# C-B products of units 4 to 7 in two row groups in turn, the second in the bank of y, under new due times

## The chip, the core and the metric

The kernel runs on one core of a Trainium2 chip. Five engines work from queues of their own: TensorE (PE in the profile, PEld its weight loads), VectorE (DVE), ScalarE (ACT), GpSimd (POOL) and SyncE (SP, which issues all DMAs here). The metric is the device time of one execution in microseconds; less is better.

## What is computed

Three stages in a row, all in fp32 at the interface. A chunked linear scan ("attention") over 4 batches, 8 heads, 768 steps; then an MLP with an ELU; then a second MLP in which two products are multiplied by each other.

```python
# scan, per chunk; cum = cumulative log decay in the chunk
CB = einsum('bhin,bhjn->bhij', Cc, Bc)          # the C-B product
M = CB * L                                      # L = exp(cum_i - cum_j), causal
y = einsum('bhij,bhjd->bhid', M, xc) + einsum('bhin,bhnd->bhid', Cc, state) * exp(cum)
state = decay_full * state + sum_j Bx_j
# MLP 1: 3072 tokens, 256 -> 2048 -> 256
h = x @ w_in;  g = where(h > 0, h, exp(min(h, 0)) - 1);  x = g @ w_out
# MLP 2: 3072 tokens, 256 -> 1536 -> 256
x = ((x @ w_a) * (x @ w_b)) @ w_out2
```

## The kernel before

**Units.** The scan is cut into 24 units, u = 0 to 23, one for 128 steps of one batch. Four units make one token tile of 512 (n = u // 4, also called t in the MLP), and eight make a set s = u // 8. A unit has these steps, all in the function `unit`: loads by SP (`ld_*`); the scan of decays on DVE (`scan`, L630); the last column to `le` (`last_col`, L645, L647) and x times it on POOL (`xend`, L650); the C-B product on PE; `mask`, C-B times the decay matrix, on DVE (L686), once for each half of four heads; M, the product with x and with the state on PE (`ym`, L717, L721, L725), into `ybank`, the bank of y; the state's update (`st_up`, L739, L741); and y out of the bank as x of the MLP, on ACT and DVE (`x_w`, L757, for tile 0; `x_hi`, L760, and `x_lo`, L763, from tile 1 on).

**C-B in three forms.** Units 0 to 3 (n == 0) use `cbm2`: heads 0 to 3 stand on rows 0 to 15 of the operand tile and heads 4 to 7 on rows 32 to 47, so that the two groups use different rows of the array; their matmuls alternate, and each group has its own PSUM bank. Units 4 to 7 (s == 0, n == 1) have the same operands (fp32, 16 rows) but use `cbm` once for each group: 4 matmuls, which are 8 passes of the array in fp32, into `cbank`, and the mask of a group must have read the bank before the next one writes. Units 8 to 23 use `cbm` on bf16 operands of 128 rows, which ACT casts (L531) and SP stores (L539) and loads again (L578).

**The bank of y** holds y of a unit in columns 0 to 255, the two tiles of the new state (`dsb`) in 256 to 383, and in the last 128 the target of the fillers: `warm` (L369), bf16 matmuls of zeros.

**MLP 1.** Tile 0 uses the weights in plain fp32 (L783, two passes a matmul). From tile 1 on each fp32 value is split into two fp32r parts, and a product is three matmuls (L792, L793, L795 for up, L804, L805, L808 for down). The work goes in pairs of 128 hidden columns: up into one of two up tiles of two banks (`up_115`, `up_116` in the rows, pairs alternate), exponential on ACT (`ex`, L890), minus one (`em`, L894), the ELU's choice on DVE (`gg`, L900, into `e_86` and others), hi and lo parts (`hi` L904, `lo` L909 on DVE or L911 on POOL), then down into two accumulators (`acc_117`, `acc_118`). Pair p+2 writes the up tile of pair p. MLP 2 goes in groups (L1120 to L1253).

**What sets the order.** All steps are put into a list by `add`, with a planned cost on one or more engines, the steps they follow, and a due time. `Plan.emit` runs a list schedule over it: among the steps that could start, it takes the earliest start, then the earliest due time, and issues the step on the engine chosen. The result is a fixed order on each engine. The table MOVE shifts due times by part ("unit", 4) and step ("cbm"). Where PE would stand idle by the plan before FILL_TO = 50 us, `emit` puts in fillers through `plan.fill`. On the chip each engine follows its order and waits on semaphores.

Of the kernel before, what the change touches and what calls it, by code (L numbers as in the profile page):

```python
# [17 lines left out]
P = 128  # L18
# [31 lines left out]
    ("bc", (0, 2, 1)): {"": 3.2, "rest": -2.7},  # L50
    ("bc", (1, 2, 0)): {"rest": 2.4},
    ("late", 1): {"rest": -2.9},
    ("late", 3): {"": -1.4, "comb": 1.7, "high_s": 3.6},
    ("late", 4): {"": 2.6, "high": 2.5},
    ("late", 6): {"": -5.0, "comb": 3.2},
    ("late", 8): {"": -20},
    ("pair", (1, 3)): {"": -2.5},
    ("pair", (3, 3)): {"": -1.3},
    ("pair", (3, 5)): {"": 1.0},
    ("pair", (3, 6)): {"": 0.6},  # L60
    ("pair", (4, 0)): {"": -2.1},
    ("split", ("w_in", 2)): {"": -4.1},
    ("split", ("w_in", 3)): {"": 5.8},
    ("split", ("w_out", 0)): {"high": -1.3},
    ("split", ("w_out", 1)): {"high": 5.2},
    ("split", ("w_out", 3)): {"": -1.3},
    ("unit", 0): {"scan": -2.0},
    ("unit", 1): {"ld_x": 2.0},
    ("unit", 10): {"": 5.1, "ld_x": -0.4, "x_lo": -0.4},
    ("unit", 11): {"st_up": 0.1},  # L70
    ("unit", 12): {"": 7.3, "ld_sm": 1.4, "mask": 4.4},
    ("unit", 13): {"": -3.7},
    ("unit", 14): {"ld_sm": -1.5},
    ("unit", 15): {"": 1.6, "<lambda>": -1.2, "xend": 4.0, "ym": 4.4},
    ("unit", 16): {"cbm": 0.8, "st_bd": 1.3},
    ("unit", 17): {"x_lo": 4.1},
    ("unit", 18): {"<lambda>": -5.5},
    ("unit", 19): {"cbm": 0.5},
    ("unit", 2): {"scan": -0.3},
    ("unit", 20): {"": -4.2, "<lambda>": -1.0, "st_bd": -1.1},  # L80
    ("unit", 21): {"": 7.1, "mask": -5.0, "scan": 2.8},
    ("unit", 22): {"": 2.7, "ld_sm": -1.6, "ld_x": 1.7},
    ("unit", 23): {"": 1.9, "ld_a": 2.0, "scan": 1.7},
    ("unit", 3): {"cbm": 2.6, "last_col": 3.1, "mask": -0.9},
# [3 lines left out]
    ("unit", 9): {"": -3.0, "st_up": -3.3},
    ("w", ("w_in", 0)): {"sign": -1.0},
    ("w", ("w_in", 2)): {"put": -2.4},  # L90
    ("w", ("w_in", 3)): {"load": -1.7},
    ("w", ("w_out", 1)): {"sign": -0.6},
    ("w", ("w_out", 2)): {"": 2.4},
    ("wb", ("w_a", 0)): {"last3": -1.1},
    ("wb", ("w_a", 1)): {"": 7.0},
    ("wb", ("w_a", 2)): {"load": -5.3, "scale": 3.3, "sign": 0.4},
    ("wb", ("w_b", 2)): {"": 2.4},
    ("wb", ("w_out2", 1)): {"": 3.2, "put": 4.0, "shift": -3.9},
    ("wb", ("w_out2", 2)): {"": 6.1, "shift": 1.8},
    ("xset", 1): {"": 11.1},  # L100
    ("xset", 2): {"": 10.6, "f_t3": -8.8, "x_h": 1.6, "x_l": 6.0},
# [1336 lines left out]
```

## Time and profile before

| | us |
|---|---|
| median of 3 runs | 628.99 (628.84 to 629.89) |
| the profiled execution | 627.92 |
| its span | 626.2 |
| PE busy | 619.4 |
| DVE, ACT, POOL busy | 392.6, 372.4, 342.8 |

The profiled execution is one run by itself; its span leaves out what lies around the first and the last instruction on the engines. In a timeline an instruction's time begins when it enters the engine and its end is modelled, so of back-to-back matmuls the distance from one start to the next is the cost, and the second column, which counts the last one's drain, is a little more.

### The profile page before, as it was taken

How to read it: one execution, taken by the hardware profiler on the slowest of the kernel's cores; microseconds unless marked ns; L12 is line 12 of the kernel's file. 1: busy time of each engine (PE TensorE's matmuls, PEld its weight loads, DVE VectorE, ACT ScalarE, POOL GpSimd, SP SyncE). 2: the span in 40 equal slices, each digit the busy share in tenths (PEclk: the TensorE clock that was granted, in tenths of full speed). 3: DMA queues.
4: the chain of work that ended last, by engine and by line, in shares of the span. 5: the costliest groups of instructions: out<-in, count | busy, mean ns of one | idle time of the engine just before them, and what ended most of it. 6: DMA issues, size and time to landing. Idle time of an engine off the chain costs nothing. (4 is left out here: it accounts for less than half of the span.)

```text
span 626.2 us, 9495 instructions
## 1 busy us (share of the span) xinstructions
PE 619.4 (99%) x3658; PEld 485.3 (77%) x3658; DVE 392.6 (63%) x525; ACT 372.4 (59%) x528; POOL 342.8 (55%) x260
## 2 busy tenths in 40 slices
PE   9999999999999999999999999999999999999997
PEld 8955556788777788777888888888888888788885
DVE  7876686787876987887753766346533446433333
ACT  2375747647676776756678655557544456554443
POOL 2233465246764586546637476557655666555552
PEclk9999999999999999999999999999999999999999
DMA  6968622657668766410000000000100000100001
GB/s 194 337 198 268 208 66 92 223 173 269 214 201 299 269 211 188 152 51 1 1 1 0 2 0 1 0 1 1 68 0 2 2 0 1 68 2 0 1 0 68
DMA packets 33405, 59.96 MB, mean 96 GB/s; under 512 B 2736, under 2 KB 13904, under 8 KB 33360
## 3 DMA queue, kind: packets, MB, share of 16 engines
q1 hardware_dynamic: 33360, 59.35, 28.9%
q8 instruction: 29, 0.48, 0.3%
q14 instruction: 16, 0.13, 0.1%
HBM read 47.61 MB, written 11.73 MB: 95 GB/s over the span
## 5 line engine op out<-in xcount | busy, mean ns | idle before, releaser
L1209 DVE TENSOR_TENSOR x<-x 128x512 f32<-128x512 f32 x36 | 31.7, 884 | 82.5 <-POOL x L1253 82.0
L911 POOL TENSOR_TENSOR gl<-e,gh 128x1024 fp32r<-128x1024 f32 x20 | 50.9, 2545 | 29.1 <-ACT gh L904 21.9
L1215 POOL TENSOR_TENSOR gl<-x,gh 128x512 fp32r<-128x512 f32 x35 | 48.8, 1395 | 32.9 <-ACT gh L1212 32.9
L1253 POOL TENSOR_TENSOR x<-e,x 128x512 f32<-128x512 f32 x36 | 46.3, 1304 | 31.6 <-ACT e L1192 29.4
L804 PE MATMUL acc<-gh,hi_w_out 128*128 128x512 f32 x160 | 63.4, 396 | 0.0
L805 PE MATMUL acc<-gh,lo_w_out 128*128 128x512 f32 x160 | 62.4, 390 | 0.0
L890 ACT ACTIVATE e<-up 128x1024 f32<-128x1024 f32 x44 | 45.1, 1024 | 26.2 <-PE up L795 18.8
L630 DVE TENSOR_TENSOR_SCAN ab<-ab,delta 128x512 f32<-128x512 f32 x36 | 53.6, 1514 | 0.0
L808 PE MATMUL acc<-gl,hi_w_out 128*128 128x512 f32 x160 | 51.3, 397 | 0.1
L894 ACT ACTIVATE e<-e,bias 128x1024 f32<-128x1024 f32 x44 | 50.7, 1153 | 1.0
L900 DVE SCALAR_TENSOR_TENSOR up<-e,up 128x512 f32<-128x512 f32 x40 | 27.7, 692 | 24.8 <-ACT e L894 24.1
L1215 POOL TENSOR_TENSOR gl<-p,gh 128x512 fp32r<-128x512 f32 x18 | 23.9, 1327 | 30.8 <-issue 25.9
L792 PE MATMUL up<-xh,hi_w_in 128*128 128x512 f32 x96 | 39.4, 410 | 0.6 <-DVE gl L909 0.6
L1200 DVE TENSOR_TENSOR p<-acc,p 128x512 f32<-128x512 f32 x36 | 24.6, 690 | 24.5 <-PE acc L1182 23.2
L900 DVE SCALAR_TENSOR_TENSOR e<-e,up 128x512 f32<-128x512 f32 x48 | 30.7, 679 | 11.6 <-ACT e L894 11.4
L1121 PE MATMUL up<-gh,lo_w_out 128*128 128x512 f32 x96 | 37.5, 391 | 0.0
L793 PE MATMUL up<-xh,lo_w_in 128*128 128x512 f32 x96 | 37.5, 390 | 0.0
L1120 PE MATMUL up<-gh,hi_w_out 128*128 128x512 f32 x96 | 37.4, 390 | 0.0
L493 POOL TENSOR_TENSOR m<-m,raw 128x1024 int32<-128x1024 int32 x10 | 26.0, 2605 | 16.9 <-DVE m L483 13.9
L805 PEld LDWEIGHTS acc<-gh,lo_w_out 128*128 128x128 f32 x160 | 30.1, 188 | 5.9
L804 PEld LDWEIGHTS acc<-gh,hi_w_out 128*128 128x128 f32 x160 | 30.0, 188 | 5.9
L686 DVE TENSOR_TENSOR ab<-cbank,ab 128x512 f32<-128x512 f32 x37 | 25.3, 683 | 13.4 <-PE cbank L683 12.6
(306 smaller groups left out, 1731.9 us busy)
## 6 DMA issues: line engine op xcount, KB each, us to landing
ab<-a_seg SPq DMA_DIRECT2D x18, 512.0 KB
parts<-raw SPq DMA_DIRECT2D x64, 128.0 KB
sm<-parts SPq DMA_DIRECT2D x16, 512.0 KB
p<-in_xb SPq DMA_DIRECT2D x20, 256.0 KB
raw<-in_w_out SPq DMA_DIRECT2D x4, 1024.0 KB
fx<-in_w_out SPq DMA_DIRECT2D x3, 1024.0 KB
out_t<-m SPq DMA_DIRECT2D x12, 256.0 KB
raw<-in_w_in SPq DMA_DIRECT2D x2, 1024.0 KB
```

The lines of the kernel that those rows point to most:

```text
L630: nc.vector.tensor_tensor_scan(lt[:, h4].rearrange(flat), lt[:, h4].rearrange(flat) if n else flat4(sp[g]), delta.rearrange(flat), 0.0, op ...
L792: nc.tensor.matmul(ps, w_mm(name, whi, f, c), xh[:, c, :], start=(c == 0), stop=False)
L793: nc.tensor.matmul(ps, w_mm(name, wlo, f, c), xh[:, c, :], start=False, stop=False)
L804: nc.tensor.matmul(accs[m], w_mm(name, whi, f, m), gh, start=(f == 0), stop=False)
L805: nc.tensor.matmul(accs[m], w_mm(name, wlo, f, m), gh, start=False, stop=False)
L808: nc.tensor.matmul(accs[m], w_mm(name, whi, f, m), gl, start=False, stop=(f == last))
L890: nc.scalar.activation(gf, u, AF.Exp)
L894: nc.scalar.activation(gf, gf, AF.Identity, bias=bias[:, 0:1])
L900: nc.vector.scalar_tensor_tensor(u[:, k, :] if on_dve else gf[:, k, :], gf[:, k, :], 0.0, u[:, k, :], op0=ALU.min, op1=ALU.max)
L911: nc.gpsimd.tensor_sub(gl.ap, gf, gh.ap.bitcast(F32))
L1215: eng[e].tensor_sub(tap("l" + w), tap(wa), tap("h" + w).bitcast(F32))
L1253: eng[e].tensor_add(tap(w), tap(v), tap(w))
```

## The change

Units 4 to 7 take `cbm2` too. The second group's bank is that of y, so the step takes (waits for) the users of `cbank`, of the bank of y and of both state tiles in it; the masks of the second group read the bank of y. When unit 4's C-B is issued, fillers end. The planned costs of several PE steps are changed, and MOVE is replaced altogether: its 52 entries go and 96 others come (two shown of each). The arithmetic is the same.

```diff
 MOVE = {
-    ("unit", 4): {"": 1.9, "cbm": -3.5, "mask": 0.4},
-    ("unit", 7): {"": 1.6, "ym": -2.8},
...
+    ("unit", 4): {"cbm2": 20, "mask": -6.7},
+    ("unit", 8): {"": -1.6, "<lambda>": 3.2, "ld_a": 1.9, "ld_x": 9.7, "scan": -5.7},
...
-        i_cbs = None
-        if n == 0:
+        if s == 0:
+
+            if n:
+                cb_ = [cbb, yb]
+            cap = [flat4(x) for x in cb_]
 
             def cbm2(e):
+                if n:
+                    plan.fill = None
                 for h in range(4):
                     for g in range(2):
                         q = slice(h * P, (h + 1) * P)
                         t = sm32[row + 32 * g:row + 32 * g + N]
-                        nc.tensor.matmul(flat4(cb_[g])[:, q], t[:, 0, q], t[:, 1, q], start=True, stop=True)
-
-            i_cbs = add({"PE": 0.95}, cbm2, cb_[0].take(), cb_[1].take(), i_sm, due=due, weight=0.25)
+                        nc.tensor.matmul(cap[g][:, q], t[:, 0, q], t[:, 1, q], start=True, stop=True)
+
+            old = cb_[0].take() + cb_[1].take() + (dsb[0].users + dsb[1].users if n else [])
+            i_cbs = add({"PE": 1.1 if n == 0 else 1.25}, cbm2, old, i_sm, due=due, weight=0.25)
             smu.users.append(i_cbs)
+        else:
+            cb_ = [cbb, cbb]
         for g in range(2):
             h4 = slice(4 * g, 4 * g + 4)
 
-            cb = cb_[g] if n == 0 else cbb
-
-            def cbm(e, g=g, cbank=cb.ap):
+            def cbm(e, g=g):
                 for h in range(4):
-                    if s == 0:
-                        q = slice(h * P, (h + 1) * P)
-                        t = sm32[row + 32 * g:row + 32 * g + N]
-                    else:
-                        q = slice((4 * g + h) * P, (4 * g + h + 1) * P)
-                        t = sm.ap
-                    nc.tensor.matmul(cbank[:, h, :], t[:, 0, q], t[:, 1, q], start=True, stop=True)
+                    q = slice((4 * g + h) * P, (4 * g + h + 1) * P)
+                    nc.tensor.matmul(cbank[:, h, :], sm.ap[:, 0, q], sm.ap[:, 1, q], start=True, stop=True)
...
-            if n:
-                i_cb = add({"PE": 0.28 if s else 0.88}, cbm, cb.take(), i_sm, due=due, pad=pd, weight=1.0 if s else 0.125)
+            if s == 0:
+                i_cb = i_cbs
+            else:
+                i_cb = add({"PE": 0.31}, cbm, cbb.take(), i_sm, due=due, pad=pd)
                 smu.users.append(i_cb)
...
-                i1.append(add({"PE": 0.86}, dn_w, i_h, i_m[wk], d, i1, due=due))
+                i1.append(add({"PE": 0.92}, dn_w, i_h, i_m[wk], d, i1, due=due))
...
-            i_u.append(add({"PE": 0.88}, up_h, d_u, i_u, i_x[t][2 * q:2 * q + 2], i_m["w_in", 0],
+            i_u.append(add({"PE": 0.92}, up_h, d_u, i_u, i_x[t][2 * q:2 * q + 2], i_m["w_in", 0],
...
-                i_u.append(add({"PE": 1.72}, up_a, d_u, i_u, i_x[t], i_m[wk], due=due + 0.1 * k))
+                i_u.append(add({"PE": 1.84}, up_a, d_u, i_u, i_x[t], i_m[wk], due=due + 0.1 * k))
```

The table has 44 rows more, so a line of the new file stands some 44 to 49 lines further down: L666 of before is L715, L717 is L762, L721 is L766, L783 is L828, L792 is L837, L890 is L935, L369 is L413. PE has 176 fillers instead of 190: in the old order the last 12 stand ahead of pair 2's up, in the new order the last 18 stand between M of unit 3 and the first full up, and none follows.

PE at pair 2's up (`m_104` is the second quarter of w_in), the order before, from the end of the fillers:

```order
L783 MATMUL up_115<-x_93,m_104 128x512 x2
L683 MATMUL cbank<-sm_76 128x128 x4
L783 MATMUL up_115<-x_93,m_104 128x512 x2
L783 MATMUL acc_117<-e_86,m_103 128x512
L783 MATMUL acc_118<-e_86,m_103 128x512
L717 MATMUL ybank<-p_74,sbd 32x128 x4
L721 MATMUL ybank<-f_hi_w_out_99,p_74 32x128 x4
L717 MATMUL ybank<-p_74,sbd 32x128 x4
L721 MATMUL ybank<-f_hi_w_out_99,p_74 32x128 x4
L725 MATMUL ybank<-xe,p_74 32x64 x4
```
and in the changed kernel, from the last two of unit 4's C-B matmuls:

```order
L715 MATMUL cbank<-sm_76 128x128
L715 MATMUL ybank<-sm_76 128x128
L828 MATMUL up_115<-x_93,m_104 128x512 x4
L762 MATMUL ybank<-p_74,sbd 32x128 x4
L766 MATMUL ybank<-f_hi_w_out_99,p_74 32x128 x4
L762 MATMUL ybank<-p_74,sbd 32x128 x4
L766 MATMUL ybank<-f_hi_w_out_99,p_74 32x128 x4
L770 MATMUL ybank<-xe,p_74 32x64 x4
L828 MATMUL acc_117<-e_86,m_103 128x512
L828 MATMUL acc_118<-e_86,m_103 128x512
```
Unit 4's C-B (8 matmuls that alternate between `cbank` and `ybank`) stands whole ahead of that up, where the second half stood in its middle; its first half stood ahead of the first full up.

ACT at the exponentials of pair 0 (`up_115` to `e_86`); `m_105` is a part of w_out whose scaling is one step. Before:

```order
L890 ACTIVATE e_86<-up_115 128x1024
L894 ACTIVATE e_86<-e_86,bias 128x1024
L645 COPY le_82<-f_hi_w_out_99 128x8
L475 ACTIVATE m_105<-raw_72 128x1024
L890 ACTIVATE e_87<-up_116 128x1024
```
and in the changed kernel:

```order
L935 ACTIVATE e_86<-up_115 128x1024
L519 ACTIVATE m_105<-raw_72 128x1024
L939 ACTIVATE e_86<-e_86,bias 128x1024
L689 COPY le_82<-f_hi_w_out_99 128x8
L532 ACTIVATE raw_72<-raw_72 128x1024
L935 ACTIVATE e_87<-up_116 128x1024
```
The scaling of `m_105` has moved between the exponential of pair 0 and the step behind it.

SP at the start of the program (`sm`: C-B operands, `p`: x of a unit, `raw_72` the first weight quarter). Before:

```order
L588 DMA sm_76<-in_bc 16x1024 x2
L571 DMA p_74<-in_xb 128x512
L466 DMA raw_72<-in_w_in 128x2x1024
L588 DMA sm_76<-in_bc 16x1024 x2
L571 DMA p_75<-in_xb 128x512
```
and in the changed kernel:

```order
L632 DMA sm_76<-in_bc 16x1024 x2
L615 DMA p_75<-in_xb 128x512
L632 DMA sm_76<-in_bc 16x1024 x2
L615 DMA p_74<-in_xb 128x512
L510 DMA raw_72<-in_w_in 128x2x1024
```
The second unit's x is loaded ahead of the first one's, and the first weight load comes behind all four instead of the first two.

## Rows read from the trace of the kernel before

**Rows 1.** The page: busy us (share of the span) x instructions; tenths in 40 slices.
```profile
PE 619.4 (99%) x3658; PEld 485.3 (77%) x3658; DVE 392.6 (63%) x525; ACT 372.4 (59%) x528; POOL 342.8 (55%) x260
...
PE   9999999999999999999999999999999999999997
...
PEclk9999999999999999999999999999999999999999
```

**Rows 2.** Waits of PE: engine, line, releaser; total us, times, longest us.
```profile
PE ybank L369 <- POOL zt L365: 1.1, 1, 1.1
PE up L792 <- DVE gl L909: 0.6, 1, 0.6
PE up L1124 <- POOL gl L1215: 0.4, 1, 0.4
PE cbank L683 <- DVE ab L686: 0.2, 1, 0.2
```

**Rows 3.** Timeline of PE, 30 to 84 us: start us, us, engine, line, operation, tiles, count.
```profile
30.49 1.15 PE L683 MATMUL cbank<-sm 16*128 16x128 f32 x8
31.57 5.43 PE L783 MATMUL up<-x,m 128*128 128x256 f32 x16
36.84 0.83 PE L369 MATMUL ybank<-zt 128*128 128x128 bf16 x12
37.51 1.94 PE L783 MATMUL up<-x,m 128*128 128x512 f32 x4
39.37 1.15 PE L683 MATMUL cbank<-sm 16*128 16x128 f32 x8
40.46 1.98 PE L783 MATMUL up<-x,m 128*128 128x512 f32 x4
...
48.21 3.70 PE L783 MATMUL up<-x,m 128*128 128x512 f32 x8
51.84 1.15 PE L683 MATMUL cbank<-sm 16*128 16x128 f32 x8
...
61.63 3.60 PE L783 MATMUL up<-x,m 128*128 128x512 f32 x8
65.16 1.15 PE L683 MATMUL cbank<-sm 16*128 16x128 f32 x8
...
82.78 1.15 PE L683 MATMUL cbank<-sm 16*128 16x128 f32 x8
83.86 1.12 PE L783 MATMUL acc<-e,m 128*128 128x512 f32 x2
```

**Rows 4.** Groups of PE, 30 to 90 us: busy us, mean ns, idle before.
```profile
L683 PE MATMUL cbank<-sm 16*128 16x128 f32 x64 | 9.2, 283 | 0.0
```

**Rows 5.** Timeline of PE, 11 to 14 us: unit 0's C-B and the next step.
```profile
11.38 1.16 PE L666 MATMUL up<-sm 16*128 16x128 f32 x16
12.47 1.72 PE L606 MATMUL acc<-a,delta 128*128 128x128 f32 x13
```

**Rows 6.** Timeline of ACT, then of DVE, 32 to 38 us: pair 0's gate, a mask.
```profile
33.60 1.02 ACT L890 ACTIVATE e<-up 128x1024 f32<-128x1024 f32 x1 [2.49 <-PE up L783]
34.66 1.15 ACT L894 ACTIVATE e<-e,bias 128x1024 f32<-128x1024 f32 x1
...
35.81 1.16 ACT L475 ACTIVATE m<-raw 128x1024 f32<-128x1024 f32 x1
...
32.57 1.22 DVE L630 TENSOR_TENSOR_SCAN f_hi_w_out<-f_hi_w_out,delta 128x512 f32<-128x512 f32 x1
35.84 1.28 DVE L900 SCALAR_TENSOR_TENSOR e<-e,up 128x512 f32<-128x512 f32 x2 [2.05 <-ACT e L894]
37.04 0.68 DVE L686 TENSOR_TENSOR f_hi_w_out<-cbank,f_hi_w_out 128x512 f32<-128x512 f32 x1
```

**Rows 7.** Timeline of PE at its three later waits, and what follows.
```profile
174.31 0.38 PE L683 MATMUL cbank<-sm 128*128 128x128 bf16 x4 [0.18 <-DVE ab L686]
...
203.70 0.47 PE L792 MATMUL up<-xh,hi_w_in 128*128 128x512 f32 x1 [0.63 <-DVE gl L909]
204.00 0.39 PE L793 MATMUL up<-xh,lo_w_in 128*128 128x512 f32 x1
...
533.18 0.73 PE L1124 MATMUL up<-gl,op_x 128*128 128x512 f32 x2 [0.44 <-POOL gl L1215]
```

**Rows 8.** Timeline of PE, ACT, DVE, 45 to 47 us: y of unit 4.
```profile
44.98 0.29 PE L725 MATMUL ybank<-xe,p 128*32 128x64 f32 x8
45.21 1.98 PE L783 MATMUL acc<-e,m 128*128 128x512 f32 x4
...
45.66 0.34 ACT L760 CAST xh<-ybank 128x256 fp32r<-128x256 f32 x1
...
46.03 0.28 DVE L741 SCALAR_TENSOR_TENSOR state<-state,db,ybank 128x64 f32<-128x64 f32 x1
46.23 0.42 DVE L763 TENSOR_TENSOR xl<-ybank,xh 128x256 fp32r<-128x256 f32 x1
```

**Rows 9.** Timeline of PE, first 10.3 us: fillers L369, spread of unit data L606.
```profile
1.06 3.49 PE L369 MATMUL ybank<-zt 128*128 128x128 bf16 x31 [1.06 <-POOL zt L365]
4.34 3.02 PE L606 MATMUL acc<-a,delta 128*128 128x128 f32 x16
...
8.38 2.05 PE L606 MATMUL acc<-a,delta 128*128 128x128 f32 x16
10.27 0.50 PE L369 MATMUL ybank<-zt 128*128 128x128 bf16 x6
```

**Rows 10.** Timeline of ACT, SP, PE, 99 to 115 us: unit 8's operands.
```profile
103.15 0.61 ACT L531 CAST raw<-raw 128x512 bf16<-128x512 f32 x1
...
99.52 5.45 SPq L539 DMA_DIRECT2D parts<-raw  x8
107.85 0.90 SPq L578 DMA_DIRECT2D sm<-parts  x2
...
114.46 0.40 PE L683 MATMUL cbank<-sm 128*128 128x128 bf16 x4
```

**Rows 11.** Windows of 1 us: length, busy (x) by engine, PEclk, DMA share, GB/s.
```profile
109.00:110.00 1.00, 1.00 (x6) 0.82 (x5) 1.00 (x3) 0.97 (x2) 0.00 (x0) 1.00 0.37 127
110.00:111.00 1.00, 1.00 (x6) 0.84 (x5) 1.00 (x1) 0.76 (x1) 0.00 (x0) 1.00 1.03 401
```

More of the change, by code (lines that the diff above doesn't have):

```diff
@@ L49 @@
 MOVE = {
[L50 to L84, printed above, removed]
-    ("unit", 4): {"": 1.9, "cbm": -3.5, "mask": 0.4},
@@ L86 @@
-    ("unit", 5): {"x_lo": -2.4},
-    ("unit", 7): {"": 1.6, "ym": -2.8},
[L88 to L101, printed above, removed]
+    ("bc", (0, 1, 0)): {"": 1.4, "load": -1.3},
+    ("bc", (0, 2, 1)): {"": -11.6},
+    ("bc", (1, 2, 0)): {"": -9.3, "rest": 3.7},
+    ("bc", (1, 2, 1)): {"rest": -8.8},
+    ("group", 0): {"": -5.3, "dn_h": 1.5, "mm3": 0.3},
+    ("group", 10): {"": -1.9, "gg": 0.4},
+    ("group", 11): {"": -5.7},
@@ new lines @@
+    ("group", 12): {"": 2.5},
+    ("group", 2): {"": 1.7},
+    ("group", 3): {"": -3.9, "dn_h": -1.1, "gg": 5.6},
+    ("group", 4): {"mm3": 2.6},
+    ("group", 5): {"dn_h": 0.8, "mm3": 1.6},
+    ("group", 6): {"mm3": -1.9},
+    ("late", 2): {"": -17.0, "high": -5.8},
+    ("late", 3): {"high_s": 11.9},
+    ("late", 5): {"": -14.2},
+    ("late", 6): {"": -11.4, "rest": -17.5},
+    ("late", 7): {"": 6.3, "high": -10.0},
+    ("late", 8): {"": -0.9},
+    ("pair", (0, 2)): {"gg": -3.3},
+    ("pair", (0, 4)): {"": 0.9, "up_a": -6.9},
@@ new lines @@
+    ("pair", (0, 5)): {"dn_w": 1.6},
+    ("pair", (0, 6)): {"dn_w": 3.0},
+    ("pair", (0, 7)): {"dn_w": 1.6},
+    ("pair", (1, 0)): {"dn_w": -2.6},
+    ("pair", (1, 5)): {"": 1.2, "up_a": -0.6},
+    ("pair", (2, 0)): {"": -12.7, "hi": -1.1},
+    ("pair", (2, 1)): {"up_a": -2.0},
+    ("pair", (2, 2)): {"dn_h": 2.2, "lo": -2.2},
+    ("pair", (2, 4)): {"dn_h": -1.2},
+    ("pair", (2, 6)): {"up_a": -2.2},
+    ("pair", (2, 7)): {"": -3.4, "up_a": -3.6},
+    ("pair", (3, 0)): {"": -2.7, "dn_h": -0.9},
@@ new lines @@
+    ("pair", (4, 6)): {"dn_h": 7.0},
+    ("pair", (5, 1)): {"dn_0": 3.5, "up_a": 1.1},
+    ("pair", (5, 2)): {"dn_l": 2.2, "up_a": 2.0},
+    ("pair", (5, 3)): {"": -0.8, "em": 0.5},
+    ("pair", (5, 4)): {"up_a": -10.4},
+    ("pair", (5, 5)): {"dn_l": -0.5},
+    ("pair", (5, 6)): {"dn_h": 3.2},
+    ("pair", (5, 7)): {"dn_l": -1.9},
+    ("split", ("w_in", 0)): {"rest": -1.6},
+    ("split", ("w_in", 1)): {"high": 4.4},
+    ("split", ("w_in", 2)): {"": 4.7, "high": -0.1, "rest": 4.8},
+    ("split", ("w_in", 3)): {"high": -0.3},
@@ new lines @@
+    ("split", ("w_out", 0)): {"": 1.8},
+    ("split", ("w_out", 1)): {"": 12.0, "rest": -2.8},
+    ("split", ("w_out", 2)): {"": 10.7},
+    ("unit", 0): {"": -5.5, "ld0": 5.7, "ld_x": 8.5},
+    ("unit", 1): {"": -11.1},
+    ("unit", 11): {"x_lo": -0.5, "ym": -8.7},
+    ("unit", 12): {"": -19.7, "scan": 20},
+    ("unit", 13): {"": -17.6, "ld_x": 14.8},
+    ("unit", 14): {"": -10.3, "<lambda>": 2.5, "ld_x": -20},
+    ("unit", 15): {"": 1.8, "ld_db": -7.4, "scan": -10.0},
+    ("unit", 17): {"<lambda>": -4.0, "cbm": 6.4, "xend": -7.2},
@@ new lines @@
+    ("unit", 18): {"": -3.2, "scan": 3.5, "st_bd": 2.1, "x_lo": 15.0},
+    ("unit", 19): {"<lambda>": -5.2, "scan": 1.5, "st_up": 5.3},
+    ("unit", 21): {"": 4.7, "cbm": -3.4, "scan": 1.0, "st_bd": 10.4, "ym": 5.0},
+    ("unit", 22): {"cbm": -4.9},
+    ("unit", 23): {"": 5.7, "cbm": 9.6, "ld_x": -3.7},
+    ("unit", 3): {"st_up": -3.1},
+    ("unit", 4): {"cbm2": 20, "mask": -6.7},
+    ("unit", 5): {"<lambda>": 1.1, "ld_a": 5.3},
+    ("unit", 6): {"": -5.4},
+    ("unit", 7): {"": 2.4},
@@ new lines @@
+    ("unit", 8): {"": -1.6, "<lambda>": 3.2, "ld_a": 1.9, "ld_x": 9.7, "scan": -5.7},
+    ("unit", 9): {"": 3.0, "ld_a": 2.1, "scan": -5.9},
+    ("w", ("w_in", 0)): {"last3": -9.8},
+    ("w", ("w_in", 1)): {"": -4.9},
+    ("w", ("w_in", 2)): {"": -2.3, "shift": -3.8, "sign": 5.7},
+    ("w", ("w_in", 3)): {"": -2.1, "load": 1.4},
+    ("w", ("w_out", 0)): {"": -19.9, "load": 1.2},
+    ("w", ("w_out", 1)): {"last3": 13.0, "put": -5.6, "sign": -6.4},
+    ("w", ("w_out", 2)): {"": 1.6},
+    ("w", ("w_out", 3)): {"": 5.8, "load": -3.8},
```

28 lines of the change are left out of this document (23 added, 5 removed).

## The prediction

> **What bounds the kernel now.** I began with the page: TensorE (PE) is busy in 99% of the span and no other engine in more than 63% [rows 1]. The next view was PE's waits by releaser, which asks whether its 1% is worth anything: four waits, 2.3 us in all, 1.1 of it before the first instruction has data [rows 2]. So time can leave this kernel almost only with PE's own instructions or with the gaps between them, and the PE timeline was read next. The span is 626.2 and the profiled execution took 627.92; the rest of 1.7 us lies around it, and the tail behind the last matmul has the same order in both kernels. All sums below are against 627.92, and are then set on the median of the runs, 628.99, which is 1.07 higher.
>
> In the timeline one thing stands out between 30 and 84 us. A C-B block of units 4 to 7 (8 passes of 16 rows, one row group, one bank) takes 1.15 us and the next instruction starts 1.08 to 1.09 behind it: 30.49 to 31.57, 39.37 to 40.46, 82.78 to 83.86 [rows 3]. There are 8 such blocks, 64 instructions [rows 4]. Ahead of them the trace shows the other form: unit 0's C-B goes to both row groups in turn, two banks, 16 passes, and the next instruction starts 1.09 behind it, 11.38 to 12.47 [rows 5]. Twice the passes cost the same time, since two stand in the array at once. Mean of one is 283 ns in the slow form while they are issued at 1.09/8 = 136 ns; in the alternating form 68 ns.
>
> **The change part by part.**
>
> *Blocks.* Eight blocks become four of 16 passes: 8 × 1.085 − 4 × 1.09 = 4.3 us of PE time gone.
>
> *Switches.* The array must change its form of tiling on both sides of a block. Eight L783 passes between two blocks last 3.63 (48.21 to 51.84), and 3.53 with a block on one side only (61.63 to 65.16) [rows 3]; so one side costs 0.10, a block 0.20, and four blocks fewer give 0.8. Together a block fewer is worth 1.28, four are worth 5.1.
>
> *Fillers.* 190 become 176, and none stands behind unit 4's C-B any more, because the bank of y is in use there. Fillers are issued where PE would wait anyway, so I cost them at nothing: the cover is the wait itself. The 12 at 36.84 lasted 0.67 and stood ahead of the pair-2 up, which needs pair 0's gate product out of its bank: that ended at 37.12, and the up started at 37.51 [rows 3, 6]. If all 14 were pure loss, 14 × 0.056 (0.67/12) = 0.8 would be gained: an end of the range.
>
> *The start.* The C-B block of 1.08 that stood ahead of the first full up moves behind it, and 18 fillers (1.0 us) stand there instead; SP's queue moves the first weight load behind two more loads. In ACT's order the scale of m_105 now stands between the exponentials of pair 0 and their second pass. That scale took 1.16 at 35.81 [rows 6]. So pair 0's gate product, which ended 37.12, is 1.16 later against its up; its up can start at most 1.08 earlier (30.49 for 31.57). It ends at about 37.2 and the pair-2 up starts 0.39 behind it, as before: 37.6 instead of 37.51. PE gets there with both halves of unit 4's C-B done (30.5 + 5.27 for the ups + 1.28 = 37.05), and waits some 0.5 with no filler. By 37.6 it is thus one block ahead; from there 7 blocks stood in the old order and 3 stand in the new one: four blocks, 5.1, less 0.1. If the first up comes as late as before, 31.57, it loses another 1.1: an end of the range.
>
> *Due times anew.* This moves steps on all engines and adds no arithmetic. M (the product with the masks) stands directly beside a C-B block once less often, which costs a switch, 0.1. The waits of the later stages are small: 0.18, 0.63 and 0.44 at 174.3, 203.7 and 533.2 [rows 7], 1.25 together. The new order brings some up products closer to the pair two before them, whose gate must be out of the bank: the shortest distance in PE work, counted from the order, falls from 7.5 us to about 4.6 (pair 2 of the last tile), and an ACT-ACT-DVE chain of 1.02 + 1.15 + 1.28 = 3.45 [rows 6] fits into it with little over. I keep the old waits and add one of their mean size, 0.4. Bounds: −1.25 (all go) and +1.25 (as many again).
>
> *Waits for the bank of y.* Unit n+1's second C-B half now needs that bank, and M of a unit needs it back. In the trace y of unit 4 is written until about 45.2 and read by ACT at 45.66 and DVE at 46.03 and 46.23, so it is free at 46.65 [rows 8], 1.4 us behind M. By the order the next C-B stands behind eight or more L783 passes after M in each case, 3.4 us at 0.43 each. The other way too at least eight passes, 3.4, lie between a C-B and the M behind it, against two masks of 0.68 on DVE [rows 6], 1.36. I cost this at nothing; the cover is those up and down products, and without it each of the seven turns (four to M, three back) would cost 1.4.
>
> **Sum:** −4.3 −0.8 +0.1 +0.1 +0.4 = −4.5. That is 623.4 against 627.92 and **624.5** against the median.
>
> *One rule weighed.* The trace has two row groups at work at a time only in two banks; in unit 0 these are cbank and a bank of up [rows 5]. The new pair, cbank with the bank of y, is again two banks, and by these rows keeps the 1.09. The Trainium skill, "TensorEngine Tiling (Array Packing)", Gotcha 1, says that different row tiles cannot use the same PSUM bank at a time and that software must keep them apart. By it the change is allowed as it stands, and the sum stays −4.5; what it speaks against is any overlap of a C-B half with M in the bank of y, since both come from row tiles. If that costs waits, the sum is that of the first rival, −1.3.
>
> **The rivals.**
>
> (a) *The bank of y becomes the bound.* C-B of units 5 to 7 and M of units 4 to 7 each wait for the other's readers. For: one bank now serves two producers, and DVE has other work that can stand ahead of the readers. Against: the distances above. If a gate product of 1.28 and a scan of 1.22 [rows 6] come first, a turn costs 1.36 + 2.5 − 3.4 = 0.46, and seven 3.2: −4.5 + 3.2 = −1.3, so 627.7.
>
> (b) *Everything gained.* Old waits gone and the removed fillers real: −4.5 − 0.4 − 1.25 − 0.8 = −6.95, so 622.0. For: due times are set for the whole program again. Against: the waits of before are spread and small, and new ones can come with a new order.
>
> (c) *The clock falls.* The same L606 runs at 0.184 each from 4.34 (2.95 us for 16) and at 0.118 from 8.38 (1.89 for 16) [rows 9], although the page's clock row reads 9 tenths all along: PE worked at the lower of its two levels (1.2 instead of 2.4 GHz) until some 6 us, after an idle start. That stretch lost about 2.6 us: 31 fillers in 3.28 instead of 31 × 0.056 = 1.74, and 2.95 − 1.89 = 1.06. With no filler behind unit 4, a fall at 37 us would give that back: −1.9, 627.1. Against: PE idled 0.63 at 203.07 and the next passes kept their 0.23 us [rows 7]. The Trainium skill, "TensorE: Matmul & The Clock Gate", Part 1, has the clock fall after idle time and rise again with work; the trace agrees at its start, and shows no fall after this gap of 0.63.
>
> (d) *Slower: unit 8's operands arrive late.* PE now reaches the split stage 4.6 us earlier. C-B of unit 8 needs operands that ACT casts, SP stores and SP loads again: last cast at 103.15, eight stores from 99.52, load issued at 107.85, and PE used it at 114.46 [rows 10]. DMA traffic begins at about 109 again and has carried 0.13 + 0.40 MB by 111 [rows 11], the 512 KB of that load: it landed near 111.0. In the new order that C-B stands 16 split passes earlier besides, 16 × 0.23 = 3.6: 114.5 − 4.6 − 3.6 = 106.3. If the casts move along with PE by 4.7 or more, nothing waits. If ACT takes the two passes of one more exponential first (1.02 + 1.15 [rows 6]) and the last cast ends 2.2 later than before, the data land at 113.2 and PE waits 6.9 in one piece: −4.5 + 6.9 = +2.4, so 631.4. It costs something from a last cast at 98.4 and makes the kernel slower from about 103, its time of before. For: ACT's last cast comes from a chain POOL-ACT of its own, which doesn't run faster because PE does. Against: in the new order the casts stand earlier among ACT's exponentials. All that ends slower gets 0.08, with this as the dearest single wait.
>
> **How the numbers follow.** Forecast (between −3.2 and −5.9) 0.70; (b) 0.07; (a) 0.08; (c) 0.03; milder waits with −1.3 to −3.2 left 0.02; no change 0.02; slower 0.08. The bound for a difference is 0.2%, 1.26 us, about what a measurement of this kernel can tell from none. Of (a), half lies within that bound: faster 0.70 + 0.07 + 0.04 + 0.03 + 0.02 = 0.86, same 0.04 + 0.02 = 0.06, slower 0.08. For the range: below, (b) in great part, 622.4; above, (a) and (c), 627.8. The likeliest case alone spans 623.1 to 625.8.
>
> **What would show it.** Right: four L715 blocks of 16 passes at 1.09 each, no wait on them for readers of the bank of y over 0.2; first L837 of the split stage 4 to 5 us before 92.6; PE's waits at 1 to 2.5 us without the start; PE busy at about 615. A pair-2 up at 37.3 to 37.9, with an idle stretch of up to 0.6 ahead of it, released by DVE's gate product. Wrong: blocks at 2 us (row groups not together), waits of M for masks, a wait before unit 8's C-B (bank free, operands late), or passes of L783 longer than 0.43 behind 37 us.

## The result, and the profile after

| | before | after |
|---|---|---|
| median, us | 629.12 (628.84 to 629.89, 4 runs) | 621.73 (621.28 to 623.18, 4 runs) |
| profiled execution | 627.92 | 621.71 |
| its span | 626.2 | 620.0 |
| PE busy | 619.4 | 613.1 |
| last pair of matmuls starts | 621.20 | 614.99 |

The ratio of the runs is 0.9885, 95% interval 0.9866 to 0.9903: 7.2 us (6.1 to 8.4) less; the medians lie 7.4 apart. The forecast was 624.5 with a range down to 622.4: the direction was right, the size too small, and the time fell 0.7 below the range. In the two profiled executions the difference is 6.2.

The page after, in the lines that answer to [rows 1]: PE is the bound as before, at the same clock, with 6.3 us less of work and gaps.

```profile
PE 613.1 (99%) x3644; PEld 481.0 (78%) x3644; DVE 391.2 (63%) x527; ACT 374.1 (60%) x531; POOL 340.7 (55%) x255
...
PE   9999999999999999999999999999999999999997
...
PEclk9999999999999999999999999999999999999999
```

PE's waits, as in [rows 2] (the columns are the total, the times, the longest): the three late waits of 0.6, 0.4 and 0.2 are gone, one of 0.8 is new, and one of 0.6 stands ahead of fillers.

```profile
PE ybank L413 <- POOL zt L409: 1.1, 1, 1.1
PE cbank L728 <- DVE ab L731: 0.8, 1, 0.8
PE ybank L413 <- ACT x L802: 0.6, 1, 0.6
```

PE's timeline at the places of [rows 3]. Unit 4's C-B is now one block of 16 passes that come in pairs, 36.12 and 36.13 the first; the pair-2 up follows at 37.34. The other three blocks come in pairs too, and the next step starts 1.09 behind each (71.52 to 72.61, unit 7's). The first split pass stands at 87.36 where it stood at 92.61, and the last row of matmuls at 614.99 where it stood at 621.20.

```profile
28.45 0.64 PE L766 MATMUL ybank<-f_lo_w_out,f_lo_w_out 128*32 128x128 f32 x16
...
29.81 1.17 PE L413 MATMUL ybank<-zt 128*128 128x128 bf16 x18 [0.60 <-ACT x L802]
30.82 5.38 PE L828 MATMUL up<-x,m 128*128 128x256 f32 x16
36.12 0.37 PE L715 MATMUL cbank<-sm 16*128 16x128 f32 x1
36.13 0.37 PE L715 MATMUL ybank<-sm 16*128 16x128 f32 x1
...
37.34 3.67 PE L828 MATMUL up<-x,m 128*128 128x512 f32 x8
40.95 0.32 PE L762 MATMUL ybank<-p,sbd 128*32 128x128 f32 x4
...
45.70 0.37 PE L715 MATMUL cbank<-sm 16*128 16x128 f32 x1
...
71.52 0.37 PE L715 MATMUL cbank<-sm 16*128 16x128 f32 x1
...
72.61 3.70 PE L828 MATMUL up<-x,m 128*128 128x512 f32 x8
...
87.36 0.80 PE L837 MATMUL up<-xh,hi_w_in 128*128 128x512 f32 x1
...
614.99 0.61 PE L1169 MATMUL up<-gl,op_x 128*128 128x512 f32 x2
```

The same two places in the kernel before:

```profile
92.61 0.79 PE L792 MATMUL up<-xh,hi_w_in 128*128 128x512 f32 x1
...
621.20 0.61 PE L1124 MATMUL up<-gl,op_x 128*128 128x512 f32 x2
```

Three milestones cut the 6.2 us into stages. The first full up came at 31.57 and now at 30.82: 0.75 less. From there to the first split pass it was 61.04 and is 56.54: 4.50 less. From that pass to the last pair of matmuls it was 528.59 and is 527.63: 0.96 less. Run 1, the kernel before again, has 30.96, 61.03 and 529.57 for the three. So the middle stage is firm, while 0.75 and 0.96 hang on which execution of before is taken: by run 1 they are 0.14 and 1.94.

ACT and DVE at pair 0, as in [rows 6]. The scale of m_105 does stand between the two passes of the exponential; the gate product ends at 37.19 and the up starts at 37.34, 0.1 behind the earliest that PE's own order allows. Both masks of unit 4 are done by 38.67, M starts at 40.95: the bank of y is free with 2.3 to spare. The other way it was closer: DVE takes the last of unit 4's y out of the bank at 44.93, behind a scan of 1.98, and ends at 45.32, and unit 5's C-B writes there from 45.70 on: 0.4 to spare.

```profile
32.80 1.02 ACT L935 ACTIVATE e<-up 128x1024 f32<-128x1024 f32 x1 [3.04 <-PE up L828]
33.72 1.13 ACT L519 ACTIVATE m<-raw 128x1024 f32<-128x1024 f32 x1
34.74 1.14 ACT L939 ACTIVATE e<-e,bias 128x1024 f32<-128x1024 f32 x1
...
35.91 1.28 DVE L945 SCALAR_TENSOR_TENSOR e<-e,up 128x512 f32<-128x512 f32 x2 [0.34 <-ACT e L939]
37.38 0.69 DVE L731 TENSOR_TENSOR f_hi_w_out<-cbank,f_hi_w_out 128x512 f32<-128x512 f32 x1 [0.19 <-PE ybank L715]
37.99 0.68 DVE L731 TENSOR_TENSOR f_hi_w_out<-ybank,f_hi_w_out 128x512 f32<-128x512 f32 x1
...
44.93 0.39 DVE L808 TENSOR_TENSOR xl<-ybank,xh 128x256 fp32r<-128x256 f32 x1
```

The one late wait that this view still names, by its rows: the start moves 1.14 behind the matmul ahead, 0.91 more than the 0.23 of a pass.

```profile
176.46 0.39 PE L850 MATMUL acc<-gh,lo_w_out 128*128 128x512 f32 x1
177.60 0.38 PE L728 MATMUL cbank<-sm 128*128 128x128 bf16 x4 [0.75 <-DVE ab L731]
```

Unit 8's operands, as in [rows 10]: the last cast came 6.9 earlier than before and the load was issued 7.4 earlier, while PE used it 8.9 earlier: 1.5 of the old margin is gone, and nothing waited.

```profile
96.28 0.60 ACT L575 CAST raw<-raw 128x512 bf16<-128x512 f32 x1
...
100.48 0.90 SPq L622 DMA_DIRECT2D sm<-parts  x2
...
105.56 0.40 PE L728 MATMUL cbank<-sm 128*128 128x128 bf16 x4
```

### The profile page after: what moved, and what is told of

Read it like the earlier page. It is cut to its first block, busy times and chain, and to the rows that moved or that the text cites. A ratio compares the mean times of both kernels' runs of the same rounds, so it can differ in the third digit from the quotient of the medians.

```text
span 620.0 us, 9471 instructions
## 1 busy us (share of the span) xinstructions
PE 613.1 (99%) x3644; PEld 481.0 (78%) x3644; DVE 391.2 (63%) x527; ACT 374.1 (60%) x531; POOL 340.7 (55%) x255
## 4 chain that ended last, share of the span: by engine, by line
PE 98%; DMA 1%; ACT 0%; DVE 0%; SPq 0%; issue 0%; POOL 0%; POOLq 0%
PE acc L849 6%; PE acc L853 6%; PE up L837 6%; PE acc L850 6%; PE up L838 6%; PE up L840 6%; PE up L1166 5%; PE up L1165 5%; PE up L1169 5%; PE up L828 5%; PE acc L828 5%; PE acc L1226 4%; PE acc L1225 4%; PE acc L1227 4%; PE ybank L1226 3%; PE cbank L1226 3%
## 5 line engine op out<-in xcount | busy, mean ns | idle before, releaser
L1254 DVE TENSOR_TENSOR x<-x 128x512 f32<-128x512 f32 x36 | 28.0, 779 | 79.2 <-POOL x L1298 78.7
L935 ACT ACTIVATE e<-up 128x1024 f32<-128x1024 f32 x44 | 45.1, 1026 | 39.2 <-PE up L840 31.6
L674 DVE TENSOR_TENSOR_SCAN ab<-ab,delta 128x512 f32<-128x512 f32 x36 | 50.4, 1418 | 2.0 <-DMA ab<-a_seg 2.0
L837 PE MATMUL up<-xh,hi_w_in 128*128 128x512 f32 x96 | 39.6, 412 | 0.0
L1257 ACT CAST gh<-x 128x512 fp32r<-128x512 f32 x36 | 22.4, 622 | 19.2 <-DVE x L1254 19.2
```

The lines of the kernel that those rows point to most:

```text
L837: nc.tensor.matmul(ps, w_mm(name, whi, f, c), xh[:, c, :], start=(c == 0), stop=False)
```

## The experiments

Each was run beside the kernel before on the same chip; the chip is another one for each group of four. Medians of before were 628.92 in the first four, 629.09 in the next four, 628.30 in the last four; its single runs lay between 627.13 and 630.35, so differences under 1 us between medians are read with care. PE's waits are those behind 85 us in the profiled execution; a wait costs PE somewhat more than its idle time (0.91 for 0.75 in the row at 177.60).

| run | median, us | ratio to before (95%) | first full up | PE's waits |
|---|---|---|---|---|
| before | 629.12 | 1 | 31.57 | 1.2 |
| after | 621.73 | 0.9885 (0.9866 to 0.9903) | 30.82 | 0.8 |
| 1 before again | 629.14 | 1.0001 (0.9992 to 1.001) | 30.96 | 2.1 |
| 2 pairs, old due times | 633.62 | 1.0079 (1.0059 to 1.0098) | 32.39 | 8.3 |
| 3 old C-B, new due times | 631.91 | 1.0051 (1.0038 to 1.0063) | 30.85 | 4.8 |
| 4 no turns | 624.68 | 0.9935 (0.9923 to 0.9947) | 31.60 | 0.4 |
| 5 without 18 fillers | 621.68 | 0.9881 (0.9867 to 0.9895) | 30.66 | 0.3 |
| 6 fewer fillers | 619.66 | 0.9862 (0.9844 to 0.988) | 28.54 | 1.0 |
| 7 old lengths | 627.98 | 0.9996 (0.9984 to 1.0009) | 31.39 | 4.9 |
| 8 pairs, copies first | 633.94 | 1.0082 (1.0065 to 1.01) | 31.13 | 9.4 |
| 9 scan planned at 1.26 | 633.90 | 1.0094 (1.0066 to 1.0122) | 32.38 | 8.6 |
| 10 lengths 1.83, 0.915 | 628.63 | 1.0005 (0.9989 to 1.0022) | 30.95 | 4.0 |
| 11 before, fewer fillers | 626.45 | 0.9967 (0.9955 to 0.9979) | 28.82 | 2.2 |
| 12 no late fillers | 622.31 | 0.992 (0.9891 to 0.995) | 34.22 | 1.0 |

### 1. The kernel before again

No edit.

> The kernel before, unchanged. Theory 1 (its profiled execution of 627.92 lay at the fast end of its own spread): ratio 1.000 within 0.2%, runs between 628 and 630, and a new profiled execution near 629 with about 1 us more in a place that can be named. Theory 2 (profiling itself makes it faster): again near 627.9 in the profiled execution and near 629 in the others.

Measured: 629.14, eleven runs from 628.29 to 629.51, and a profiled execution of 628.29. So the execution that the forecast was summed against was at the low end, and so is this one (Theory 1). Theory 2 is not borne out by the other kernels: the profiled executions of runs 2 and 12 lie above their medians. Where the 0.8 us above it goes is not told by these two traces, since no execution at 629 was profiled. They do show what moves: the first full up stood at 31.57 in one and at 30.96 in the other, the start being that much quicker, and PE's wait for gl at about 203 us was 0.6 in the one and 1.4 in the other. What the start gains, a later wait partly takes back.

### 2. Pairs under the old due times

```diff
 # the kernel before, and in unit():
-        if n == 0:
+        if s == 0:
+            if n:
+                cb_ = [cbb, yb]
...
+                if n:
+                    plan.fill = None
```

> The kernel before with one part of the change alone: units 4 to 7 in two row groups in turn, the second in the bank of y, with the due times and planned lengths of before. Theory 1 (the pairs give four blocks and their switches, 5.1, in any order): 629.1 - 5.1 = 624.0, ratio 0.992. Theory 2 (most of the gain hangs on the due times, since the old ones leave the bank of y late): about 627, ratio 0.997, with waits of PE for DVE or ACT at the C-B blocks between 40 and 85 us.

Measured: 633.62, slower by 0.6 to 1.0%. Neither theory stands: the C-B blocks came as expected (first split pass at 88.84, 3.8 earlier than before, although the first full up was 0.8 later), and nothing waited on them. The time was lost behind. The timeline of PE, then of ACT:

```profile
105.07 0.50 PE L805 MATMUL acc<-gh,hi_w_out 128*128 128x512 f32 x1 [3.21 <-ACT x L942]
...
108.27 0.63 PE L793 MATMUL up<-xh,hi_w_in 128*128 128x512 f32 x1
108.70 0.63 PE L794 MATMUL up<-xh,lo_w_in 128*128 128x512 f32 x1
...
103.92 0.62 ACT L531 CAST raw<-raw 128x512 bf16<-128x512 f32 x1 [0.80 <-POOL raw L534]
104.44 1.07 ACT L942 COPY x<-acc 128x512 f32<-128x512 f32 x2
```

Down of tile 1 waits 3.21 for ACT to copy tile 0's accumulators (L942). On ACT the copies stand behind the last two casts of unit 8's operands, and these wait for POOL. PE's passes then take 0.43 instead of 0.23 (108.27 to 108.70): the clock has fallen. The window from 90 to 120 us (length, PE busy, granted clock, share of DMA engines, GB/s) has a granted clock of 0.89 of full speed, and from 106 to 112 it is 0.50, the lower of the two levels.

```profile
90.00:120.00 30.00, 26.02 (x92) 0.89 0.41 136
```

### 3. The old C-B under the new due times

```diff
 # the changed kernel, and in unit():
-        if s == 0:
+        i_cbs = None
+        if n == 0:
...
+            if n:
+                i_cb = add({"PE": 0.31 if s else 1.1}, cbm, cb.take(), i_sm, due=due, pad=pd, weight=1.0 if s else 0.125)
```

> The changed kernel with the old C-B of units 4 to 7 (one group after the other, in one bank) under the new due times and lengths. Theory 1 (parts add up; due times are worth the rest of 7.4 - 5.1 = 2.3): 626.8, ratio 0.9963; before the split stage eight blocks of 1.09 again. Theory 2 (the new due times are good only with the pairs): 629 or more, ratio 1.000 or over, with new waits before 90 us.

Measured: 631.91, slower by 0.4 to 0.6%. Theory 1 falls and theory 2 stands in its size, not in its place: the eight blocks are there again (1.09 each, as expected), but the waits of 4.8 us lie behind 170 us, 2.8 of them for DVE's gl. The two parts do not add up: +4.7 and +3.0 alone, −7.2 together.

### 4. The pairs without turns

```diff
-                for h in range(4):
-                    for g in range(2):
+                for g, h in [(g, h) for g in range(2) for h in range(4)] if n else [(g, h) for h in range(4) for g in range(2)]:
```

> The changed kernel with the same order on every engine, but inside each C-B block of units 4 to 7 all four heads of the first row group come before those of the second. Theory 1 (what saves time is that two passes of different row groups stand in the array at once): each block lasts 2.2 instead of 1.09, four blocks cost 4.4, so 626.1, ratio 0.9952. Rival (one block instead of two and the second bank do it; turns don't matter): 621.7, ratio 0.988.

Measured: 624.68, between the two, 2.95 above the changed kernel, of which 0.8 is a later start of this execution (first full up 31.60 for 30.82). A block lasted 1.64, not 2.2 (36.91 to 38.55):

```profile
36.91 0.82 PE L715 MATMUL cbank<-sm 16*128 16x128 f32 x5
37.46 0.37 PE L715 MATMUL ybank<-sm 16*128 16x128 f32 x1
37.57 0.27 PE L715 MATMUL cbank<-sm 16*128 16x128 f32 x1
...
37.90 0.72 PE L715 MATMUL ybank<-sm 16*128 16x128 f32 x5
38.55 1.98 PE L828 MATMUL up<-x,m 128*128 128x512 f32 x4
```

The rows show why the expectation was too high: the second group's passes (ybank) begin at 37.46, in the midst of the first group's, although the program has them behind all of those. Three pairs were formed anyway, while the rest of the first group came. A pass alone takes 0.11 (five from 36.91 to 37.57, the first longer by 0.10), a pair as much, and the two switches 0.2. So a block has 13 places of 0.11 where full turns need 8, which is the measured 0.55, and four blocks make 2.2. That two groups share the array is shown; that turns are needed for it is only half so.

### 5. Without the last 18 fillers

```diff
-        for _ in range(n):
+        for _ in range({18: 0}.get(n, n)):
```

> The changed kernel without its last 18 fillers, those between M of unit 3 and the first full up; every engine's order is otherwise the same. They began 0.60 us behind M, when ACT had x out of the bank of y, and lasted 1.0; the up needs the same x and nothing later. Theory 1 (these fillers stand where PE could work; costing fillers at nothing was wrong): 0.9 to 1.0 less, 620.8, ratio to before 0.987, and the first full up at about 29.9. Rival (they only fill a wait that another engine sets, pair 0's gate above all): 621.7. Second rival (without them the clock falls): over 623.

Measured: 621.68 against 621.73, too close to the changed kernel to be told from it with four runs each; by the median this is the rival's 621.7. The trace shows the gain at its place: the first full up starts as soon as ACT has x, 0.90 behind M's last step (L770) instead of 1.91, so these 18 fillers had cost their full 1.0. But in this execution M itself came 0.85 later, PE having waited 0.75 for a scan at 16.7 us.

```profile
29.76 0.29 PE L770 MATMUL ybank<-xe,f_lo_w_out 128*32 128x64 f32 x8
30.66 1.56 PE L828 MATMUL up<-x,m 128*128 128x256 f32 x6 [0.61 <-ACT x L802]
```

### 6. Fewer fillers in three places

```diff
-        for _ in range(n):
+        for _ in range({18: 0, 72: 48, 51: 41}.get(n, n)):
```

> The changed kernel without the last 18 fillers, with 41 instead of 51 in the stretch at 17 us and 48 instead of 72 at 24 us; the order is otherwise the same. Unit 3's masks ended 1.0 before M of unit 3 could pass the fillers, and the first half up stood 0.6 behind its weights. Theory 1 (all of that is PE's own loss): 2.3 less than the changed kernel, 619.4, ratio to before 0.985. Rival (the earlier start is lost again where later waits are set by ACT, POOL and DMAs): 620.8 to 621.7, with PE's waits between 170 and 260 us grown by what the start gained.

Measured: 619.66, 2.1 less than the changed kernel where 2.3 was expected: theory 1. Its five runs go from 618.89 to 622.41, and its interval overlaps that of the changed kernel, so the size is less sure than the direction. It has the lowest median of the study. The first full up stands at 28.54 instead of 30.82, and the waits behind 85 us are 1.0 instead of 0.8. M of unit 3 now waits 0.2 for each of the two masks, so no filler is left too many there:

```profile
26.80 0.43 PE L766 MATMUL ybank<-f_lo_w_out,f_lo_w_out 128*32 128x128 f32 x8 [0.22 <-DVE f_lo_w_out L731]
27.39 0.43 PE L766 MATMUL ybank<-f_lo_w_out,f_lo_w_out 128*32 128x128 f32 x8 [0.17 <-DVE f_lo_w_out L731]
...
28.54 1.78 PE L828 MATMUL up<-x,m 128*128 128x256 f32 x7 [0.61 <-ACT x L802]
```

### 7. The old planned lengths

```diff
-                i1.append(add({"PE": 0.92}, dn_w, i_h, i_m[wk], d, i1, due=due))
+                i1.append(add({"PE": 0.86}, dn_w, i_h, i_m[wk], d, i1, due=due))
...
-                i_u.append(add({"PE": 1.84}, up_a, d_u, i_u, i_x[t], i_m[wk], due=due + 0.1 * k))
+                i_u.append(add({"PE": 1.72}, up_a, d_u, i_u, i_x[t], i_m[wk], due=due + 0.1 * k))
```

> The changed kernel with the planned lengths of the fp32 steps as before (1.72, 0.86, 0.88 instead of 1.84, 0.92, 0.92), due times and pairs as changed. Theory 1 (the lengths keep the plan's PE in step with the chip's, and the due times were set for them; a mismatch brings waits as in the two mixed kernels): 625 or more, with waits of PE for DVE and ACT between 85 and 260 us. Rival (lengths are a detail): 621.7 within 0.2%.

Measured: 627.98, 6.3 above the changed kernel, with the first split pass at 87.83 (it was 87.36) and waits of 4.9 behind it. Theory 1 in its size; whether its reason holds is what runs 9 and 10 ask.

### 8. The copies ahead of the casts

```diff
 # run 2; in emit(), when the order is issued
+                if i == evac[1]:
+                    for j, f in held:      # unit 8's last two casts and POOL's step between them
+                        self.steps[j][1](f)
```

> The kernel with pairs under the old due times (633.6), with one thing moved: on ACT the two copies of tile 0's accumulators come ahead of the last two casts of unit 8's operands, behind which they stood; POOL's step between these casts moves with them. No engine's order changes elsewhere. Theory 1 (the old due times cost because ACT waits for POOL ahead of those copies, PE idles 3.2 us for them and then works at its lower clock): the waits of 3.2 and 0.8 shrink to 1.5 at most, the passes behind them take 0.23 instead of 0.43, about 5 us less: 628.5, ratio to before 0.999. Rival (the casts are just as urgent): PE waits 3 to 4 us for unit 8's operands at about 111 instead, 631 to 633.

Measured: 633.94, as run 2 and 0.9 above the rival's upper end: the rival. The wait for the copies is gone, down starts without it, and a little later in the order PE waits 3.48 us for unit 8's operands instead, until 112.74; soon after it the passes again take 0.42 (113.89 to 114.31).

```profile
112.74 0.40 PE L713 MATMUL cbank<-sm 128*128 128x128 bf16 x4 [3.48 <-DMA sm<-parts]
...
113.89 0.63 PE L823 MATMUL up<-xh,lo_w_in 128*128 128x512 f32 x1
114.31 1.05 PE L825 MATMUL up<-xl,hi_w_in 128*128 128x512 f32 x2
...
104.75 0.62 ACT L560 CAST raw<-raw 128x512 bf16<-128x512 f32 x1 [3.03 <-POOL raw L563]
```

ACT's last cast stands at 104.75 behind 3.03 us of waiting for POOL. It is the cast chain on POOL and ACT that is late in this order, not the order of two steps on ACT. In the changed kernel the same last cast ends at 96.9.

### 9 and 10. Two plans with planned lengths altered by a hundredth or less

```diff
-            i_scan.append(add({"DVE": 1.25}, scan, i_ab if n else i_ab[g], i_ones2, due=due, port=n > 0))
+            i_scan.append(add({"DVE": 1.26}, scan, i_ab if n else i_ab[g], i_ones2, due=due, port=n > 0))
```

> The changed kernel with one planned length altered by a hundredth: the plan takes a scan on DVE as 1.26 us instead of 1.25. Nothing that is computed changes, but 629 rows of PE's order stand elsewhere. Theory 1 (the table of due times is fitted to one exact plan, and any other plan lets ACT, POOL and DVE come late between 85 and 260 us): 625 to 629, PE's waits in the split stage 4 us or more. Theory 2 (the plan is robust, and the mixed kernels were slow because their lengths or blocks did not fit the chip): 621.7 within 0.2%.

```diff
-                i_u.append(add({"PE": 1.84}, up_a, d_u, i_u, i_x[t], i_m[wk], due=due + 0.1 * k))
+                i_u.append(add({"PE": 1.83}, up_a, d_u, i_u, i_x[t], i_m[wk], due=due + 0.1 * k))
...
```

> The changed kernel with the planned fp32 steps at 1.83 and 0.915 instead of 1.84 and 0.92; 538 rows of PE's order move. As for the altered scan: Theory 1 (fitted to one plan) 625 to 629. Theory 2 (only a real mismatch of planned and true lengths costs, as with 1.72): 621.7 within 0.3%.

Measured: 633.90 and 628.63, where the changed kernel has 621.73. Theory 1 stands in both, in run 9 with 5 us more than it allowed. A hundredth of a microsecond in a planned length costs 12 and 7 us; nothing else differs than the order, fillers included, that the list schedule makes of it. By the distances between starts run 10's late waits cost about 5.8 and the changed kernel's 1.1, most of the 6.2 between their profiled executions. The scan's kernel waits on ACT, DVE, POOL and a DMA in turn (the largest of its waits behind 85 us):

```profile
PE acc L849 <- ACT gh L949: 2.1, 2, 1.8
PE cbank L728 <- DMA sm<-parts: 1.8, 1, 1.8
PE cbank L728 <- DVE ab L731: 1.6, 2, 0.9
PE up L837 <- DVE gl L954: 1.3, 1, 1.3
```

This also settles run 7: its loss is of the size of run 10's and is no evidence on the lengths 1.72 or 1.84.

### 11. The kernel before with fewer fillers

```diff
-        for _ in range(n):
+        for _ in range({12: 12, 75: 53, 51: 30, 5: 0}.get(n, n)):
```

> The kernel before with 132 fillers instead of 190: 30 instead of 51 at 17.8 us, 53 instead of 75 at 25.5, none of the 15 in three groups of five; the order is otherwise the same. Theory 1 (fillers outlast the waits they cover, in the old kernel too): the first full up 1.5 earlier, at 30, and the kernel 627.6, ratio 0.998. Rival (later waits on POOL, DVE and DMAs take it back): 629.1, with the wait for gl at 203 us grown from 0.6 to about 2.

Measured: 626.45 against 628.30, ratio 0.9967 (0.9955 to 0.9979). The first full up came 2.75 earlier than in the profiled execution of before and 2.14 earlier than in run 1, for 58 fillers fewer: 0.037 to 0.047 each of the 0.056 that one takes, so most of their time had been PE's own. The kernel gained 1.85, 0.032 each. The rest was lost behind, in part as the rival had it: PE's wait for gl at about 203 us is 1.4, as in run 1, against 0.6 in the profiled execution of before.

```profile
28.82 1.35 PE L783 MATMUL up<-x,m 128*128 128x256 f32 x5
...
PE up L792 <- DVE gl L909: 1.4, 1, 1.4
```

### 12. No fillers behind the start

```diff
-        for _ in range(n):
+        for _ in range({18: 0, 72: 0, 51: 0}.get(n, n)):
```

> The changed kernel without the 51, 72 and 18 fillers; PE then idles about 2 us ahead of the first half up and about 3 us ahead of unit 3's M. Theory 1 (the fillers earn nothing but the clock, and gaps of 2 to 3 us let it fall): the passes behind these gaps take twice their time, the first full up at 29 or later, 620.5 to 623. Rival (gaps of this size leave the clock as it is): as the kernel with fewer fillers, 619.5.

Measured: 622.31 (621.78 to 627.06). Theory 1. The profiled execution is the slowest of the six, with a mean granted clock of 0.988; four others lie at 621.8 to 622.7 with 0.994, where the changed kernel has 0.999 or more, so they lost clock too, but less. The windows, read as in run 2, show a granted clock of 0.50, the lower of its two levels, 1.2 GHz, from 20 to 28 us, behind idle stretches of 1.6 and 2.3 us on PE, and PE's work of that stretch taking twice its time; the first full up came at 34.22.

```profile
20.00:28.00 8.00, 6.83 (x48) 0.50 1.02 340
28.00:36.00 8.00, 4.91 (x44) 0.71 0.86 247
```

## Why the prediction was right or wrong

**The block and its switches: right.** 1.28 a block was forecast. Between the first full up and the first split pass the old order had 7 blocks and 12 fillers, the new one 4 blocks: 3 × 1.28 + 0.67 = 4.51, measured 4.50. By run 4's rows a merged block saves 8 × 0.11 = 0.9 of passes; the other 0.4 is one entry and exit less, 0.2 in the block itself and 0.2 in the passes beside it.

**The start and the pair-2 up: right within 0.35, in part by luck.** Up to the first split pass the terms make −5.1 + 0.1 + 0.1 = −4.9 (the second 0.1 is the switch at unit 3's M), and the measurement is −5.25. By 37.6 the forecast had one block of gain, less 0.1; the up stood at 37.34. That pair 0's gate product ended at 37.19, as forecast, is two errors that cancel: the first full up stood 0.33 later than the 30.49 it was reckoned from, and the scale of m_105 lengthened the way from that up to the gate product by 0.82 (5.55 before, 6.37 now) and not by 1.16. PE's wait for the gate was 0.1 and not 0.5, since the 0.39 between gate and up in the old order was the end of the 12 fillers. And the step "fillers are issued where PE would wait anyway, so I cost them at nothing" is false: at their place 18 of them cost their full 1.0 (run 5), and runs 6 and 11 price one at 0.037 to 0.047 of its 0.056 by the first full up and at 0.03 to 0.04 by the medians. The rows of the old start had shown it, since unit 3's masks ended over 1 us ahead of M. The error stayed small because 32 fillers went and 18 came: the 0.67 of the last 12 is in the 4.50, and the 18 ahead of the first full up gave 1.0 back.

**Due times anew: the step that failed.** "I keep the old waits and add one of their mean size, 0.4" puts +0.4 behind the first split pass; measured is −0.96. By the distances between starts the old order lost 0.78, 0.60, 0.34 and 0.2 in its later waits, 1.9 together, and the new one 0.91 and 0.21, 1.1. That is 0.8 of the 0.96; the other 0.15 I have not followed up. So the term was mis-sized by 1.36 in these two executions, and others make it more: behind the first split pass the old order took 528.59, 529.57 and 529.73 (before, runs 1 and 11; PE's wait for gl at about 203 us is 0.6 in the first and 1.4 in the others), the new one 527.4 to 528.1 (after, runs 4, 5, 6 and 12). Each execution of the new order is quicker there than each of the old one. The term was wrong in kind too: it is no sum over moved steps. Runs 2, 3, 7, 9 and 10 show 4.0 to 8.6 of waits where the table of due times meets another plan, and the changed kernel 0.8 where it meets its own. That speaks for a table fitted to one exact plan; whether a plan that differs is good cannot be told from the sizes of its changes.

**The base.** The sum was made against 627.92 and put on a median 1.07 above it. Profiled against profiled, the gain is 6.2: 4.5 + 0.35 + 1.36. Median against median it is 7.4, and against the 628.30 that before had beside runs 9 to 12 it is 6.6. That the changed kernel's profiled execution lies on its median while that of before lies 1.2 below accounts for the rest. With the two terms right the forecast would have been 622.8, still inside the range; the last 1.1 is this base. Part of it may be the old order's wait for gl, which was at its shorter value in the execution that the sum was made against; that is not shown, and the range should have held the spread.

**The rivals.** (b), everything gained, came nearest: 622.0 for 621.73. It was made of the right parts, late waits that go and fillers that are real, but its −6.95 lies between the 6.2 of the profiled executions and the 7.4 of the medians: of its 1.25 of old waits only a balance of 0.8 went in those executions, and the base made up for it, which is luck. Its chance of 0.07 looks too small.

(a), the bank of y: no PE wait on it anywhere in the changed kernel, but it came nearer than the prediction had it. Unit 4's y was out of the bank 3.2 behind M, where the old order had shown 1.4, because a scan stood ahead on DVE, one of the two steps that (a) names; of the 3.6 us of passes 0.4 were left. The margins of the other turns are 2 us or more. What the Trainium skill, "TensorEngine Tiling (Array Packing)", Gotcha 1, asks of software, to keep different row tiles out of one PSUM bank at a time, the order gives here without a wait. The prediction took M for a row tile too; by the rows its matmuls (128*32) use all 128 rows, and no run here shows whether they could share a bank with a C-B pass.

(c), the clock: it fell in runs 2, 8 and 12, behind idle stretches of 3.2, 3.5 and 2.3 us. In the changed kernel the longest, but for the first 1.1, is the 0.8 at 177 us, and the granted clock stayed full. The Trainium skill, "TensorE: Matmul & The Clock Gate", Part 1, has the clock fall after idle time; the three runs agree.

(d), unit 8's operands late: not in the changed kernel, but run 8 is this rival in its mechanism, with a cast at 104.75, a wait of 3.48 and a slower kernel. Run 9 has the same wait, 1.8 long, under the new due times, so it is the one order made of them that keeps clear of it.

## What to carry to other kernels

Where a planner's table fixes the order on all engines, price the change of the program and the change of the plan as one, and expect a part of it alone to be slower than either; a near-equal plan can cost more than the edit brings. Warm-up matmuls are not free because a plan put them where it expected a wait: compare, in the trace, when the data behind them were ready, and cut the number until a short wait shows, but not to none, which in run 12 cost the clock. And a forecast from one profiled execution carries the spread of that execution, about 1 us of 629 here, which belongs in the range.
